# A gates' store on another queue, two transposes a block sooner, two subtractions on another engine

## The chip, the cores and the metric

The kernel runs on one core of a Trainium2 chip. Its engines have a queue of their own each and meet at semaphores: TensorE (PE; its weight loads are PEld), VectorE (DVE), ScalarE (ACT), GpSimd (POOL) and SyncE (SP), which here only issues DMAs. The metric is the device time of one execution in microseconds, as the median of several runs; less is better.

## The reference, cut to what matters

A chunked attention with a few memory keys, followed by a top-1 mixture of experts on its output.

```
attention (4 batches x 8 heads, 768 tokens, head size 64):
    for each chunk of 32 queries: keys = 8 memory keys + 16 left + own 32 + 8 right
    a = softmax(q k^T / 8);  out = a v
x = out as [3072 tokens, 512]
logits = x @ w_gate + modality_bias[modality_id];   e = argmax;   gate = softmax(logits)[e]
out[t] = gate[t] * (relu(x[t] @ w1[e]) @ w2[e])     8 experts, 512 -> 1024 -> 512
```

All of it is in float32.

## The kernel before, in words

**Attention** goes over 16 units of two heads, in two halves each, as a pipeline: scores, softmax, product with the values, transposes of the result (`xT`) for the router. The results go to a DRAM copy `xd`, each token's gate to a DRAM table `gd`. The router (`route`, one generator per batch of 768 tokens) finds each token's expert and rank and builds a table of the tokens in the order of experts. Its steps are pumped in between other work.

**Experts** are done in slots of 256 tokens of one expert. A slot gathers its rows by indirect DMA on GpSimd's queue (`gather`, `fetch`: first the rows from `xd`, then the gates from `gd`), transposes them on TensorE (`trans`: eight transposes in two sets; ScalarE casts the high part `xth`, VectorE subtracts for the low part `xtl`, L822 and L823), and multiplies twice. Each float32 product is made of three products of rounded parts: high x high, low x high, high x low. For that each block of 128x512 weights is split by `conv`: ScalarE casts the high part (L758), VectorE subtracts it from the raw weights for the low part (L759). A slot has 8 blocks of the first matrix (`raw[0..7]`) and 8 of the second (`raw[8..15]`).

`mm1_first(f)` is block f of the first product: 12 matmuls into a PSUM bank, then ScalarE's ReLU (L848) and VectorE's low part (L849). Banks come in turn from a pool of four (`bank()`); the eight blocks of slot 1 with the router's table product before block 7 take nine of them, so block 5 takes block 1's bank, block 6 block 2's, the table product block 3's and block 7 block 4's. `mm2(f)` is block f of the second product, 6 matmuls.

Slots 0 and 1 take the experts chosen after three batches, so that their work starts before the fourth batch is routed. The rest of that routing (the generator `last`, stepped by `further`) is laid between slot 0's and slot 1's blocks. It plans the slots on VectorE (`plan_slots`, its last step writes `regs1`), gets `ac` and `lo`, and then makes one-hot rows (L673, L676): for the first four of six groups on GpSimd, the others on VectorE.

**The order is the order of the code.** Each engine runs its instructions in the order in which the program was written; there is no scheduler. An instruction waits at the head of its queue, and what is behind it waits too.

**Weight loads** (`load_w(row, half)`) are issued by SP, eight at a time, into the raw buffers; they wait for the buffers to be read out by `conv`. Each carries a condition: where the expert is that of the slot before, it is issued but moves nothing. Slot 1 starts with

```
def slot(s):
    load_w(s + 1, 0)              # slot 2's first matrix, buffers 0 to 7
    ...
    for f in range(8):
        mm1_first(f)
        if f < 3: conv(5 + f)     # blocks 5 to 7 of slot 1's first matrix
        further(2)
        if f < 6: conv(8 + f)
```

so its conversions of blocks 5 to 7 stand behind slot 2's loads into these buffers; blocks 0 to 4 are converted in slot 0's second product.

Of the kernel before, what the change touches and what calls it, by code (L numbers as in the profile page):

```python
# [45 lines left out]
def tile_chunk_attention_top1_moe(  # L46
# [14 lines left out]
    nc = tc.nc  # L61
# [22 lines left out]
    def bank():  # L84
        return ps.tile([P, 512], F32, name="tr", tag="tr", bufs=4)
# [293 lines left out]
    def store_x(u):  # L379
        b, g = divmod(u, 4)  # L380
        nc.gpsimd.dma_start(xd[b * S:(b + 1) * S, g * P:(g + 1) * P].rearrange("(t p) c -> p t c", p=P), xbs[u])
# [135 lines left out]
    chosen = []  # L517
# [181 lines left out]
    def second():  # L699
        cb, eb, oha, top, ia, ib = chosen  # L700
        nc.vector.tensor_scalar(oha, rev[:, 0], ia, None, op0=ALU.is_equal)
        yield "v"
        nc.vector.tensor_scalar(top, top, 511.5, 2.0 * EMPTY, op0=ALU.is_gt, op1=ALU.mult)
        yield "v"
        nc.vector.tensor_scalar(top, top, -EMPTY, None, op0=ALU.add)
        yield "v"
        nc.vector.scalar_tensor_tensor(cb, oha, top, cb, op0=ALU.mult, op1=ALU.add)
        yield "v"
        yield from first_of(cb, top, ib, eb)
        nc.vector.tensor_scalar(ohg, rev[:, 0], ib, None, op0=ALU.is_equal)  # L710
        yield "v"
        nc.vector.tensor_scalar(noth, rev[0:64, 0], ib[0:64], None, op0=ALU.not_equal)
        yield "v"
        nc.vector.tensor_add(used, oha[0:64], ohg[0:64])
        yield "v"
        nc.vector.scalar_tensor_tensor(col0u, used, 2.0, col0, op0=ALU.mult, op1=ALU.add)
        yield "v"
        nc.vector.tensor_scalar(regsb[:, 0:1], ib[0:1], -1.0, float(E), op0=ALU.mult, op1=ALU.add)
        yield "v"
        nc.vector.tensor_tensor(regsb[:, 1:2], ia[0:1], ib[0:1], op=ALU.not_equal)  # L720
        yield "v"
        nc.vector.tensor_tensor(top[0:1], ia[0:1], ib[0:1], op=ALU.is_equal)
        yield "v"
        nc.vector.tensor_scalar(top[0:1], top[0:1], 2.0, float(E * HI), op0=ALU.mult, op1=ALU.add)
        yield "v"
        nc.vector.scalar_tensor_tensor(regsb[:, 2:3], ib[0:1], -float(HI), top[0:1], op0=ALU.mult, op1=ALU.add)
        yield "v"
# [8 lines left out]
    def load_w(row, half, part=None):  # L736
        if half == 0 and part in (None, 0):
            if row == 0:
                ev[0] = nc.values_load(regs0[0:1, 0:1], engines=[mybir.EngineType.SP], min_val=0, max_val=E - 1,
                                       skip_runtime_bounds_check_because="the place of one of 8 experts")  # L740
            else:
                r = regsb if row == 1 else (regs1 if row < NSURE else regs)[row:row + 1]
                ev[row] = nc.values_load(r[:, 0:1], engines=[mybir.EngineType.SP], min_val=0, max_val=E - 1,
                                         skip_runtime_bounds_check_because="the place of one of 8 experts, or 0")
                ev[row, "c"] = nc.values_load(r[:, 1:2], engines=[mybir.EngineType.SP], min_val=0, max_val=1,
                                              skip_runtime_bounds_check_because="a comparison gives 0 or 1")
        e = ev[row]
        kw = {} if row == 0 else {"cond": ev[row, "c"]}
        for f in range(8) if part is None else range(4 * part, 4 * part + 4):
            if half == 0:  # L750
                nc.sync.dma_start(
                    raw[f].rearrange("p (c f) -> p c f", f=P),
                    w1[ds(e, 1), :, f * P:(f + 1) * P].rearrange("o (c p) f -> p (o c) f", p=P), **kw)
            else:
                nc.sync.dma_start(raw[8 + f], w2[ds(e, 1), f * P:(f + 1) * P, :].rearrange("o p d -> p (o d)"), **kw)

    def conv(i, eng=None):
        nc.scalar.copy(wh[i], raw[i])  # L758
        (eng or nc.vector).tensor_sub(wl[i], raw[i], wh[i].bitcast(F32))  # L759
# [6 lines left out]
    def fetch(rows, part):  # L766
        for t in range(2):
            nc.gpsimd.indirect_dma_start(  # L768
                out=xg[t][:, part], out_offset=None, in_=rows, in_offset=bass.IndirectOffsetOnAxis(ap=gx[:, t:t + 1], axis=0))

    def gather(row, gates=True, between=()):
        if row < 2:
            src, reg, rows = table, regsb[0:1, 2:3] if row else regs0[0:1, 1:2], N - S
        else:
            src, reg, rows = tab_i, (regs1 if row < NSURE else regs)[row:row + 1, 2:3], N
        col = nc.values_load(reg, engines=[mybir.EngineType.Pool], min_val=0, max_val=E * HI,
                             skip_runtime_bounds_check_because="clamped to the table on chip")
        nc.gpsimd.tensor_copy(ix, src[:, ds(col, 2)])
        nc.gpsimd.tensor_scalar(gx, ix, float(rows - 1), None, op0=ALU.min)
        fetch(xd[0:rows], slice(0, DM))  # L780
        for step in between:
            step()
        if flipped(row):
            for t in range(2):
                flip(planes[t], xg[t], xpl[:, :, t * P:(t + 1) * P])
        if gates:
            fetch(gd[0:rows], slice(DM, XW))
# [27 lines left out]
    def trans(half):  # L815
        t = bank().rearrange("p (c n) -> p c n", c=2)
        for cc in range(2):
            for tt in range(2):
                c = 2 * half + cc
                nc.tensor.transpose(t[:, cc, tt * P:(tt + 1) * P], xg[tt][:, c * P:(c + 1) * P], ident)  # L820
        sl = slice(2 * half, 2 * half + 2)
        nc.scalar.copy(xth[:, sl], t)  # L822
        nc.vector.tensor_sub(xtl[:, sl], t, xth[:, sl].bitcast(F32))  # L823
# [148 lines left out]
    for i in range(n + 2):  # L972
# [118 lines left out]
        if (u, hf) == (NU - 2, 1):  # L1091
            c_ld.close()
            xp = ctx.enter_context(tc.tile_pool(name="xp", bufs=1, side="right"))
            ix = xp.tile([P, 2], I32, name="ix")
            gx = xp.tile([P, 2], I32, name="gx")
            xg = [xp.tile([P, XW], F32, name=f"xg{t}") for t in range(2)]
            xt = xp.tile([P, 4, 2, 256], F32R, name="xt")
            xth, xtl = xt[:, :, 0], xt[:, :, 1]
            w1h, w1l = [xp.tile([P, 8, 512], F32R, name=f"w1{i}") for i in range(2)]
            hh, hl = [xp.tile([P, 8, 256], F32R, name=f"h{i}") for i in range(2)]  # L1100
            for f in range(8):
                raw[f] = xp.tile([P, 512], F32, name=f"raw{f}")
                wh[f], wl[f] = w1h[:, f], w1l[:, f]
            flat = vws[1].rearrange("p h c d -> p (h c d)"), kbds[0].rearrange("p c h m -> p (c h m)")
            old = [t[:, k * 512:(k + 1) * 512] for t in flat for k in range(6)]
            raw[8:16] = old[0:8]
            load_w(0, 0, 0)
            gather(0, gates=False)
            for f in range(4, 8):
                nc.gpsimd.memset(raw[f][0:1, 0:1], 0.0)  # L1110
            load_w(0, 0, 1)
            with nc.allow_non_contiguous_dma(reason="one gate per token"):
                nc.sync.dma_start(*chosen.pop())
        elif (u, hf) == (NU - 1, 1):
            other = second()
            for f in range(8, 16):
                nc.gpsimd.memset(raw[f][0:1, 0:1], 0.0)
            load_w(0, 1)
            store_x(NU - 3)
            fetch(gd[0:N - S], slice(DM, XW))  # L1120
            store_x(NU - 2)
# [20 lines left out]
    def further(k=99, pe=False):  # L1142
        if at_pe[0] and not pe:
            return
        at_pe[0] = False
        while k > 0 and not at_pe[0]:
            at_pe[0] = next(last, "full") == "full"
            k -= 1
# [22 lines left out]
    for f in range(8):  # L1171
        if f == 2:
            further(2, True)
        mm2("av", f)
        if f < 5:
            conv(11 + f)
        if f == 5:
            load_w(1, 1)
        if f in (5, 6):
            trans(f - 5)  # L1180
        if f > 2:
            further(2)
            conv(f - 3)
    store(0)

    tails = plan_tails()
# [155 lines left out]
```

## Time and profile before

| | us |
|---|---|
| median of 3 runs (lowest, highest) | 428.49 (427.87, 429.13) |
| the profiled execution | 428.21 |
| its span, first to last instruction | 426.4 |
| PE busy | 409.3 (96%) |
| PEld busy | 341.7 (80%) |
| DVE busy | 336.3 (79%) |
| ACT busy | 299.0 (70%) |
| POOL busy | 238.5 (56%) |

Times in the rows count from the span's start. Attention fills the first 133 us; slot 0 runs from there to 161, slot 1 to 186, the other ten slots to 398. Busy shares are averages: what bounds a stage is read from the waits in that stage. In a row of the timeline the bracket is the idle time of the engine before it and what ended it.

### The profile page before, as it was taken

Reading aid. Unit: us, or ns where it says so; the run is one execution under the profiler, and the core shown is the slowest. Engines: PE = TensorE matmul, PEld = TensorE weight load, DVE = VectorE, ACT = ScalarE, POOL = GpSimd, SP = SyncE. Lnnn points to the kernel's source line nnn. Section 1 sums busy time; section 2 is a strip of 40 time slices with the busy share of each in tenths; the row PEclk is TensorE's granted clock in tenths of the full one; section 3 lists DMA queues with packets and bytes.
Section 4 is the critical chain, followed back from the end, with each engine's and each line's share of the span. In section 5 each row is a group of like instructions: output and inputs, shape, how many; then the busy total and the mean of one; then the engine's idle time right before and its main releaser. Section 6 shows DMA issues by size and latency. Waiting matters only on the chain.

```text
span 426.4 us, 11406 instructions
## 1 busy us (share of the span) xinstructions
PE 409.3 (96%) x3876; PEld 341.7 (80%) x3876; DVE 336.3 (79%) x796; ACT 299.0 (70%) x594; POOL 238.5 (56%) x320
## 2 busy tenths in 40 slices
PE   7997989999999999999999999999999999999994
PEld 4886777788767878899898888888888878888883
DVE  6889589688787788948979889767989787978750
ACT  7785868687675547557666697858878677878750
POOL 8956879669671628767753672453766076420101
PEclk9999999999999999999999999999999999999998
DMA  9788999999859710334422749959957423410101
GB/s 223 157 216 208 243 265 202 258 246 209 189 147 218 247 31 2 99 100 65 98 88 52 276 118 271 332 162 305 297 209 230 87 72 83 92 59 2 50 3 55
DMA packets 82543, 66.81 MB, mean 157 GB/s; under 512 B 50659, under 2 KB 71339, under 8 KB 82476
## 3 DMA queue, kind: packets, MB, share of 16 engines
q1 hardware_dynamic: 75276, 46.36, 45.0%
q0 software_dynamic: 6784, 19.50, 15.1%
q8 instruction: 33, 0.54, 0.6%
q14 instruction: 34, 0.28, 0.2%
q10 hardware_dynamic: 416, 0.13, 0.1%
HBM read 84.64 MB, written 12.76 MB: 228 GB/s over the span
## 4 chain that ended last, share of the span: by engine, by line
PE 52%; issue 18%; POOL 10%; DMA 10%; DVE 4%; ACT 4%; POOLq 1%; SPq 0%; ACTq 0%
PE tr L847 11%; PE sc L859 8%; PE av L859 7%; PE av L363 4%; POOL xg L768 4%; DMA out_dram<-o,ix_now 4%; PE tr L828 4%; PE sc L334 3%; ACT kbd L326 3%; PE tr L388 2%; POOL planes L793 2%; PE tr L831 2%; PE tr L298 2%; DMA vw<-in_v_dram 2%; PE tr L351 2%
## 5 line engine op out<-in xcount | busy, mean ns | idle before, releaser
L828 PE MATMUL tr<-xt,w 128*128 128x512 f32 x256 | 70.1, 395 | 0.0
L759 DVE TENSOR_TENSOR w<-raw,w 128x512 fp32r<-128x512 f32 x96 | 66.3, 735 | 4.0 <-ACT w L758 3.6
L859 PE MATMUL av<-wh,h 128*128 128x512 f32 x192 | 62.4, 398 | 0.0
L273 POOL COPY vw<-vw 24x1472 f32<-24x1472 f32 x31 | 44.1, 1423 | 21.1 <-DMA vw<-in_v_dram 19.9
L758 ACT CAST w<-raw 128x512 fp32r<-128x512 f32 x96 | 53.9, 624 | 1.5 <-DMA raw<-in_moe_w_dram 1.5
L859 PE MATMUL sc<-wh,h 128*128 128x512 f32 x160 | 51.7, 397 | 0.0
L828 PEld LDWEIGHTS tr<-xt,w 128*128 128x128 f32 x256 | 44.3, 188 | 7.3 <-DVE wl L840 0.8
L847 PE MATMUL tr<-xt,w 128*128 128x256 f32 x384 | 48.0, 284 | 0.7 <-DVE xt L823 0.7
L847 PEld LDWEIGHTS tr<-xt,w 128*128 128x128 f32 x384 | 46.8, 191 | 2.0 <-DVE xt L823 0.9
L326 ACT COPY kbd<-tr 64x672 f32<-64x672 f32 x57 | 44.6, 782 | 3.1 <-PE tr L320 1.5
L831 PEld LDWEIGHTS tr<-xt,w 128*128 128x128 f32 x256 | 39.2, 188 | 5.5
L859 PEld LDWEIGHTS av<-wh,h 128*128 128x128 f32 x192 | 36.1, 188 | 8.4 <-issue 0.2
L864 POOL DMA_INDIRECT out_dram<-o,ix_now x22 | 25.4, 1155 | 30.6 <-ACT o L863 25.2
L831 PE MATMUL tr<-xt,w 128*128 128x256 f32 x256 | 40.7, 281 | 0.0
L837 DVE TENSOR_TENSOR hs<-tr,hs 128x256 f32<-128x256 f32 x64 | 26.8, 419 | 16.6 <-ACT hs L834 14.5
L859 PE MATMUL av<-wl,h 128*128 128x512 f32 x96 | 38.1, 397 | 0.0
L838 ACT ACTIVATE h<-hs 128x256 fp32r<-128x256 f32 x64 | 26.8, 418 | 15.0 <-DVE hs L837 12.4
L768 POOL DMA_INDIRECT xg<-gd,gx x24 | 28.4, 1183 | 14.9 <-DMA gd<-gt 9.3
L859 PEld LDWEIGHTS sc<-wh,h 128*128 128x128 f32 x160 | 30.1, 188 | 7.2 <-issue 0.2
L840 DVE TENSOR_TENSOR wl<-vw,wh 128x512 fp32r<-128x512 f32 x48 | 33.2, 692 | 2.2
L841 DVE SCALAR_TENSOR_TENSOR h<-hs,h 128x256 fp32r<-128x256 f32 x64 | 28.6, 447 | 7.7 <-ACT h L838 6.8
L353 ACT ACTIVATE PT<-tr 128x384 f32<-128x384 f32 x32 | 15.8, 493 | 25.2 <-PE tr L351 25.0
(267 smaller groups left out, 914.1 us busy)
## 6 DMA issues: line engine op xcount, KB each, us to landing
raw<-in_moe_w_dram SPq DMA_DIRECT2D x96, 256.0 KB
vw<-in_moe_w_dram SPq DMA_DIRECT2D x72, 256.0 KB
k<-in_k_dram SPq DMA_DIRECT2D x16, 384.0 KB
q<-in_q_dram SPq DMA_DIRECT2D x16, 384.0 KB
xd<-xb POOLq DMA_DIRECT2D x16, 384.0 KB
kbd<-in_moe_w_dram SPq DMA_DIRECT2D x24, 256.0 KB
vw<-in_v_dram SPq DMA_DIRECT2D x32, 184.0 KB
xall<-in_moe_w_dram SPq DMA_DIRECT2D x4, 1024.0 KB
```

Source lines behind the costliest of these rows:

```text
L273: copy(vw[r0:r0 + 24, h, 1:NCH, 0:D], vw[r0 + 32:r0 + 56, h, 0:NCH - 1, 0:D])
L326: copy(dst.rearrange("p c (i j) -> p c i j", j=2)[:, :, :, j], win)
L758: nc.scalar.copy(wh[i], raw[i])
L759: (eng or nc.vector).tensor_sub(wl[i], raw[i], wh[i].bitcast(F32))
L768: nc.gpsimd.indirect_dma_start(out=xg[t][:, part], out_offset=None, in_=rows, in_offset=bass.IndirectOffsetOnAxis(ap=gx[:, t:t + 1], axis=0))
L828: nc.tensor.matmul(ph, wh[f][:, c * P:(c + 1) * P], xt[:, c].rearrange("p a n -> p (a n)"), start=(c == 0), stop=False, skip_group_check=True)
L831: nc.tensor.matmul(ph[:, 0:256], wl[f][:, c * P:(c + 1) * P], xth[:, c], start=False, stop=(c == 3), skip_group_check=True)
L837: nc.vector.tensor_add(hs, ph[:, 0:256], hs)
L840: nc.vector.tensor_sub(wl[w], raw[w], wh[w].bitcast(F32))
L841: nc.vector.scalar_tensor_tensor(hl[:, f], hs, 0.0, hh[:, f].bitcast(F32), op0=ALU.max, op1=ALU.subtract)
L847: nc.tensor.matmul(ph, w[f][:, c * P:(c + 1) * P], x[:, c, :], start=(n == 0), stop=(n == 11))
L859: nc.tensor.matmul(pos[t], x, w[8 + f], start=(f == 0 and n == 0), stop=(f == 7 and n == 2))
```

## The change

Three edits. In the last but one unit of attention the store of the third batch's gates to `gd` is issued by GpSimd and no longer by SP. In slot 0's second product slot 1's two sets of transposes come behind blocks 4 and 5, before behind blocks 5 and 6. And the subtractions that give the low parts of slot 1's weight blocks 1 and 3 are GpSimd's, no longer VectorE's.

```
                 load_w(0, 0, 1)
                 with nc.allow_non_contiguous_dma(reason="one gate per token"):
-                nc.sync.dma_start(*chosen.pop())
+                nc.gpsimd.dma_start(*chosen.pop())
...
         if f == 5:
             load_w(1, 1)
-        if f in (5, 6):
-            trans(f - 5)
+        if f in (4, 5):
+            trans(f - 4)
         if f > 2:
             further(2)
-            conv(f - 3)
+            conv(f - 3, nc.gpsimd if f in (4, 6) else None)
```

`conv(i, eng)` takes the engine for the subtraction as its second argument; the cast stays ScalarE's.

How the change stands in the engines' order. On GpSimd, between slot 1's row fetches and the fourth batch's gates; `raw_2596` to `raw_2603` are raw buffers 0 to 7, `w_2592` and `w_2593` the high and low parts. Before:

```order
L768 DMA xg_2590<-gd,gx 128x4
L673 TENSOR_SCALAR l_3172<-iota_147,lo 128x130
L676 TENSOR_SCALAR a_3173<-iota_148,ac,tokm 128x192
L673 TENSOR_SCALAR l_3176<-iota_147,lo 128x130
L676 TENSOR_SCALAR a_3177<-iota_148,ac,tokm 128x192
L628 DMA gd<-gt 128x6x4
```

and in the changed kernel:

```order
L768 DMA xg_2590<-gd,gx 128x4
L759 TENSOR_TENSOR w_2593<-raw_2597,w_2592 128x512
L673 TENSOR_SCALAR l_3179<-iota_147,lo 128x130
L676 TENSOR_SCALAR a_3180<-iota_148,ac,tokm 128x192
L673 TENSOR_SCALAR l_3183<-iota_147,lo 128x130
L676 TENSOR_SCALAR a_3184<-iota_148,ac,tokm 128x192
L759 TENSOR_TENSOR w_2593<-raw_2599,w_2592 128x512
L628 DMA gd<-gt 128x6x4
```

Block 1's subtraction stands ahead of the one-hot rows, block 3's behind the first four of them. On SP, slot 2's loads into raw buffers 2 to 5, with the queues whose semaphores they wait for. Before:

```order
L751 DMA raw_2598<-in_moe_w_dram 128x4x128 [waits DMAHW1_49,DVE_49]
L751 ISA
L751 DMA raw_2599<-in_moe_w_dram 128x4x128 [waits DMAHW2_49,DVE_49]
L751 ISA
L751 DMA raw_2600<-in_moe_w_dram 128x4x128 [waits DMAHW3_49,DVE_49]
L751 ISA
L751 DMA raw_2601<-in_moe_w_dram 128x4x128 [waits DMAHW4_49]
```

and in the changed kernel:

```order
L751 DMA raw_2598<-in_moe_w_dram 128x4x128 [waits DMAHW0_49,DVE_49]
L751 ISA
L751 DMA raw_2599<-in_moe_w_dram 128x4x128 [waits DMAHW1_49,Pool_49]
L751 ISA
L751 DMA raw_2600<-in_moe_w_dram 128x4x128 [waits DMAHW2_49,DVE_49]
L751 ISA
L751 DMA raw_2601<-in_moe_w_dram 128x4x128 [waits DMAHW3_49]
```

The load into buffer 3 waits for GpSimd and no longer for VectorE, and the loads into 4 and 5 are behind it. On VectorE, around the plan of the slots (`ng` to `sta`), the difference:

```order
 L759 TENSOR_TENSOR wl_2863<-kbd_110,wh_2862 128x512
+L823 TENSOR_TENSOR xt<-tr,xt 128x2x256
 L461 TENSOR_REDUCE ng<-own 64x1
 L462 TENSOR_SCALAR ng<-ng 64x1
...
 L468 TENSOR_TENSOR sta<-sta,noth 64x8
-L759 TENSOR_TENSOR w_2593<-raw_2597,w_2592 128x512
 L823 TENSOR_TENSOR xt<-tr,xt 128x2x256
 L470 SCALAR_TENSOR_TENSOR sta<-ohg,sta 64x8
```

The first low half of the rows now stands ahead of the plan, the second in its middle, where the first one was.

## Rows read from the trace of the kernel before

**Rows 1.** The page's busy times: engine, us, share of the span, instructions.

```profile
PE 409.3 (96%) x3876; PEld 341.7 (80%) x3876; DVE 336.3 (79%) x796; ACT 299.0 (70%) x594; POOL 238.5 (56%) x320
```

**Rows 2.** Stretches: length, then PE PEld DVE ACT POOL busy, clock, DMA, GB/s.

```profile
133.70:161.00 27.30, 27.26 (x200) 23.14 (x193) 22.35 (x79) 14.62 (x33) 10.17 (x13) 1.00 0.50 139
161.00:163.00 2.00, 1.26 (x12) 1.06 (x10) 1.90 (x8) 1.48 (x3) 1.25 (x2) 1.00 0.00 0
163.00:174.40 11.40, 11.40 (x93) 11.28 (x94) 10.50 (x25) 7.01 (x16) 10.86 (x13) 1.00 0.10 26
174.40:398.00 223.60, 223.60 (x1329) 189.04 (x1328) 183.75 (x362) 164.95 (x347) 114.70 (x142) 1.00 0.53 146
```

**Rows 3.** Timeline of PE: start, us, engine, line, operation, count, idle before.

```profile
157.21 0.60 PE L820 MATMUL tr<-ident,xg 128*128 128x128 f32 x4
...
160.89 1.34 PE L847 MATMUL tr<-xt,w 128*128 128x256 f32 x10
162.97 9.14 PE L847 MATMUL tr<-xt,w 128*128 128x256 f32 x74 [0.74 <-DVE xt L823]
171.95 0.82 PE L684 MATMUL tr<-a,l 128*128 128x192 f32 x6
172.72 1.70 PE L847 MATMUL tr<-xt,w 128*128 128x256 f32 x12
```

**Rows 4.** Timeline of ACT and DVE around the rows' halves and the plan.

```profile
157.90 0.59 ACT L822 CAST xt<-tr 128x512 fp32r<-128x512 f32 x1 [4.83 <-PE tr L820]
158.52 0.69 DVE L823 TENSOR_TENSOR xt<-tr,xt 128x512 fp32r<-128x512 f32 x1 [1.15 <-ACT xt L822]
...
161.56 0.16 DVE L646 TENSOR_TENSOR ac<-c,hi 128x6 f32<-128x6 f32 x1
...
162.24 0.68 DVE L823 TENSOR_TENSOR xt<-tr,xt 128x512 fp32r<-128x512 f32 x1
...
163.14 0.70 DVE L759 TENSOR_TENSOR w<-raw,w 128x512 fp32r<-128x512 f32 x1
```

**Rows 5.** Timeline of SP: slot 2's loads into raw buffers 3, 4, 5.

```profile
163.87 0.07 SPq L751 DMA_DIRECT2D raw<-in_moe_w_dram  x1
...
164.84 0.07 SPq L751 DMA_DIRECT2D raw<-in_moe_w_dram  x1
...
165.23 0.07 SPq L751 DMA_DIRECT2D raw<-in_moe_w_dram  x1
```

**Rows 6.** Timeline of ACT and DVE in slot 1, blocks 5, 1 and 4.

```profile
165.36 0.62 ACT L758 CAST w<-raw 128x512 fp32r<-128x512 f32 x1 [1.46 <-DMA raw<-in_moe_w_dram]
...
166.02 0.69 DVE L759 TENSOR_TENSOR w<-raw,w 128x512 fp32r<-128x512 f32 x1 [0.86 <-ACT w L758]
...
167.87 0.42 DVE L849 SCALAR_TENSOR_TENSOR h<-tr,h 128x256 fp32r<-128x256 f32 x1
...
172.25 0.42 DVE L849 SCALAR_TENSOR_TENSOR h<-tr,h 128x256 fp32r<-128x256 f32 x1
```

**Rows 7.** Timeline of POOL: the first, fourth and last of eight one-hot rows.

```profile
161.75 1.06 POOL L673 TENSOR_SCALAR l<-iota,lo 128x130 fp32r<-128x130 f32 x1 [9.36 <-DVE ac L646]
...
164.40 1.30 POOL L676 TENSOR_SCALAR a<-iota,ac,tokm 128x192 fp32r<-128x192 f32 x1
...
169.41 1.33 POOL L676 TENSOR_SCALAR a<-iota,ac,tokm 128x192 fp32r<-128x192 f32 x1
```

**Rows 8.** Groups of POOL by shape: count, busy us, mean ns of one, idle before.

```profile
L273 POOL COPY vw<-vw 24x1472 f32<-24x1472 f32 x31 | 44.1, 1423 | 21.1 <-DMA vw<-in_v_dram 19.9
...
L676 POOL TENSOR_SCALAR a<-iota,ac,tokm 128x192 fp32r<-128x192 f32 x10 | 11.3, 1131 | 0.0
...
L248 POOL TENSOR_TENSOR rows_b<-bias_b,ident 24x192 f32<-24x192 f32 x1 | 0.5, 505 | 0.1
...
L246 POOL TENSOR_TENSOR bias_b<-bias_b 24x8 f32<-24x8 f32 x1 | 0.2, 196 | 0.0
```

**Rows 9.** Waits from 120 to 200 us: us in total, times, longest.

```profile
POOL xg L768 <- DMA gd<-gt: 9.3, 1, 9.3
```

## The prediction

> **What bounds the kernel now.** I read the page's first part, then the table of stretches, and only then the rows around the change. TensorE's row on the page has 409.3 us busy of 426.4 [rows 1]. A matmul's end is modelled, so that row alone proves little; the stretches say more. From 133.7 to 161 us TensorE has 27.26 of 27.30 us busy, from 163 to 174.4 all of 11.40, and from 174.4 to 398 all of 223.60, at a granted clock of 1.00 [rows 2]. Between them, from 161 to 163, it has 1.26 of 2.00: a hole of 0.74 us, the only one from the start of the expert slots to the last one's end. The reader is to see two things in this. A gain here can come only from that hole (and 0.04 us before it). And nothing behind 174.4 can absorb a delay: what slot 1 loses arrives at the end of the kernel.
>
> The timeline of TensorE shows what the hole is: slot 1's first block starts at 160.89, runs 10 matmuls and then waits 0.74 us for VectorE's `xt`, line 823 [rows 3]. This is the low half of the second pair of row transposes. VectorE starts it at 162.24, although ScalarE's half was ready long before, because in its own order the plan of the slots (up to `ac`, at 161.56) and a weight subtraction stand in front [rows 4].
>
> **The two sets of transposes, one block sooner.** They leave one place and enter another: 8 transposes and 24 matmuls in another order, no instruction more. The first set goes from 157.21 to one block sooner, about 155.8, and the second to about 157.6, that is where the first stood plus the first's own 0.4 us. ScalarE took 0.69 us from the start of a set to its cast (157.21 to 157.90) and VectorE another 0.62 (158.52) [rows 3, 4]. So the last low half now starts at 157.6 + 0.69 + 0.62 = 158.9 and is done by 159.6, before TensorE asks for it, at 162.97 - 0.74 = 162.2 [rows 3]. The hole closes: -0.74 us. What is late next? The plan rows used to follow the first `xt`, which started at 158.52; now they follow the second, at 158.9. So `ac` ends at 161.72 + 0.4 = 162.1, and GpSimd's one-hot rows, which wait for it, start 0.4 us later. The gathered rows should be there: GpSimd had issued all of slot 1's fetches by 161.75 - 9.36 = 152.4 [rows 7], 3.4 us before the new place.
>
> **The subtraction of block 1 (f = 4) on GpSimd.** VectorE loses one 0.70 us instruction. On GpSimd it stands in front of the one-hot rows, where GpSimd idled 9.36 us [rows 7]. It can run when ScalarE has cast the high half, about 157.7 (the first set's cast ends at 156.5 + 0.6, and its own cast takes 0.6), and is over by 160.7 even at the dearest price below. TensorE reads block 1's low part 16 matmuls behind 160.89, at about 162.8. Cost zero; the cover is GpSimd's idle time before `ac`, and it ends at 162.1.
>
> **The subtraction of block 3 (f = 6) on GpSimd.** This is the one that counts. It stands behind the first four one-hot instructions, and those wait for `ac`. Before, VectorE did it at 163.14, done at 163.84 [rows 4]. Now the four rows start at 162.1; they took from 161.75 to 165.70 [rows 7], of which I take back 0.05 because two of VectorE's subtractions beside them are gone, so the subtraction starts at 166.0.
>
> Its price is not in the trace at this size. GpSimd's two-operand rows took 196 ns at 8 elements and 505 at 192 [rows 8]: 309 ns for 184 more elements, 1.68 ns each, so 505 + 320 x 1.68 = 1.04 us at 512. Bounds: at the pace of its plain copy (1423 ns for 1472 elements) 0.5 us; at the pace of its two-scalar row (1131 ns for 192) 3.0 us [rows 8]. I take 1.04, the rows of the same operation. It ends at T = 167.05 (166.5 to 169.0).
>
> The Trainium skill, GPSIMD Engine Reference, section 3.1, speaks against this edit: it has a two-operand add on GpSimd at 1.96 times VectorE's time, 4497 ns for 2048 elements; a quarter is an estimate of 1.12 us. By that page the sum below would be 0.1 us longer; no run here shows the operation at this size yet.
>
> Who waits for it? Two. First TensorE: it reads that block's low half 40 matmuls after 160.89. With 74 matmuls in 9.14 us [rows 3] one is 0.123, so at 165.8; it would stall 1.3 us. Second, and longer, SP. Slot 2's weight loads go into the same raw buffers in the order 0 to 7, and the load into buffer 3 now waits for GpSimd. In the trace that load is issued at 163.87, right behind VectorE's 163.84; then 164.84 (behind subtraction 4) and 165.23, so 0.39 us from one free load to the next [rows 5]. ScalarE's cast of block 5 for slot 1 stands behind the load into buffer 5: its row waits 1.46 us for a DMA into `raw` and starts at 165.36, 0.13 after that load's issue [rows 6]. That the loads move next to nothing (26 GB/s in the stretch [rows 2]) doesn't help: the wait is for their turn. Now the issues are at 167.08, 167.47 and 167.86, and the cast starts at 167.99 (T + 0.94): 2.63 us late.
>
> What is queued behind this cast? ScalarE's next casts and ReLUs, in order, and VectorE's subtraction 5 (166.02 before), from which VectorE runs without a gap to the low half of block 4, 172.25 + 0.42 = 172.67 [rows 6]. Blocks share four PSUM banks, and block 7 takes the one that block 4 leaves: in the trace TensorE starts block 7 at 172.72 [rows 3], 0.05 after that. VectorE has no gap there to give up, so all of it moves by 2.63, and block 7 starts at 175.35. TensorE's stalls on the way (1.3 at block 3, 1.4 at block 5 for block 1's bank, freed by the row at 167.87, the rest at blocks 6 and 7) are parts of this and not added to it: it arrives at block 7 2.63 us late, net of the 0.74 gained.
>
> GpSimd's second pair of one-hot rows ended at 170.74 with TensorE asking at 171.95 [rows 3, 7]; both move by about the same (1.35 and over 2), so this costs nothing.
>
> **The gates' store on GpSimd's queue.** SP loses one issue; GpSimd gains one, in front of the touches of the buffers that SP loads next. GpSimd waited 9.3 us for this store to land before it could fetch slot 0's gates [rows 9]; part of that goes, and the stores of attention's last rows behind the fetch start sooner. But TensorE had 0.04 us to gain in the 27 us that follow [rows 2], which is the bound below zero. A loss would need SP's next loads to come later by the touches than they came by SP's own issue, which is gone; I see none and cost the edit at 0.
>
> **Sum.** +2.63 against the profiled execution's 428.21 is 430.8. The median of the runs shown is 428.49, 0.28 more, so I forecast 431.1 us. With the price's bounds the delay is 2.1 to 4.6.
>
> **Rivals.** A: the load's wait is not on the path (block 7 doesn't need what it looks like), and only TensorE's own wait for block 3 counts: 1.3 - 0.74 = +0.6, 429.1 us. For it: block 7 and the end of block 4's row stand 0.05 apart, which could be chance. Against: ScalarE's wait for the DMA is named in the trace. B, the other side: GpSimd's subtraction is done in time and the hole's 0.74 us is gained, 427.8 us. It decides at T = 165.36 - 0.94 = 164.4, so the one-hot rows would have to be over by 163.4, 2.3 us sooner than in the trace; against it is their wait for `ac`. For it: VectorE is freed of two subtractions of 0.70. C: GpSimd needs 3.0 us as in its slowest row, T = 169.0, +4.6, 433.1 us. For it: its rows beside VectorE's subtractions are stretched (1.30 against a mean of 1.13); against: VectorE's next subtraction itself waits on this one, so it runs alone.
>
> The Trainium skill, SBUF — State Buffer, "Who interferes with whom", calls the port that GpSimd shares with VectorE an exclusive lock, taken against two-input VectorE instructions. The row of 1.30 us agrees; were one to come ahead of subtraction 3, the sum would grow by its 0.70 us, to 431.8.
>
> **How the numbers follow.** Forecast (delay of 1.6 to 3.4 us) 0.68, A 0.12, B 0.06, C and in between 0.14. From no change this kernel can be told at about 0.3%, 1.3 us: A lies within it, and so does B unless VectorE's relief adds half a microsecond more, to which I give 0.04 of its 0.06. So faster 0.04, same 0.14, slower 0.82. The range, 429.3 to 432.9, leaves out B, half of A and the far end of C.
>
> **What would show it.** In the profile of the changed kernel: no wait for `xt` before slot 1's third group; GpSimd's subtraction 3 between 166 and 167.2; SP's load into buffer 3 right behind it; ScalarE's cast of block 5 at about 168.0 with a longer wait for `raw`; TensorE's stretch from 163 to 177 with some 3 us idle, at blocks 3 and 5 above all; and from there everything 2.6 later. Wrong if that cast starts before 166, or if TensorE reaches slot 1's second product (174.26 before) in under 1.3 us more.

## The result and the profile after

The changed kernel takes 430.36 us (median of 22 runs, 428.94 to 434.88), the kernel before beside it 428.33 (22 runs, 425.75 to 431.01). The ratio of the runs is 1.0073, with a 95% interval of [1.0054, 1.0092]: about 3.1 us more (2.3 to 3.9). The two medians stand 2.03 apart, so the size is known to about 1 us only. The forecast was 2.63 more. All ratios here leave out, as slow, a run over 1.5% above the fastest of its kernel: two of experiment 9 (432.54 and 433.36 us) and one of the kernel before (1374.79).

The profiled execution took 433.25 us, its span is 431.5. This is not the number to compare: its first matmul of the experts comes at 135.72, before at 133.76, so 1.96 us were lost in attention, ahead of everything that the change touches in the experts. They are not the change's: in this execution TensorE waits 1.64 us up to 78.03 us, and behind that the granted clock is 0.50, the lower of its two levels (1.2 GHz), for 3.4 us (78.5 to 81.9); the trace before has no such stretch in attention, and the first of the three edits comes some 50 us later. Over the twelve traces of this document that first matmul comes between 130.61 and 136.09. I compare from the first matmul of slot 0's second product to that of slot 1's second product: 29.03 us (150.02 to 179.05) against 26.20 (148.06 to 174.26), 2.83 more. The page's busy times, to be laid beside [rows 1], tell little:

```profile
PE 411.1 (95%) x3876; PEld 342.4 (79%) x3876; DVE 338.2 (78%) x794; ACT 300.0 (70%) x594; POOL 237.6 (55%) x323
```

Stretches of the changed kernel: slot 0, slot 1's first product, the rest (columns as in [rows 2]).

```profile
135.70:162.40 26.70, 26.70 (x195) 23.11 (x192) 22.21 (x73) 15.37 (x33) 11.09 (x14) 1.00 0.47 154
162.40:179.05 16.65, 13.28 (x103) 12.45 (x102) 12.31 (x36) 7.86 (x18) 12.89 (x15) 1.00 0.11 34
179.05:403.00 223.95, 223.95 (x1331) 189.34 (x1330) 185.72 (x362) 165.65 (x347) 110.82 (x141) 1.00 0.52 145
```

All of the loss is in the middle one: 16.65 us with 3.37 idle. Behind it TensorE is busy throughout, so nothing gives the time back. TensorE there, the answer to [rows 3]:

```profile
162.41 4.94 PE L847 MATMUL tr<-xt,w 128*128 128x256 f32 x40
168.97 2.66 PE L847 MATMUL tr<-xt,w 128*128 128x256 f32 x20 [1.62 <-POOL w L759]
173.13 1.70 PE L847 MATMUL tr<-xt,w 128*128 128x256 f32 x12 [1.50 <-DVE h L849]
175.05 1.70 PE L847 MATMUL tr<-xt,w 128*128 128x256 f32 x12 [0.22 <-DVE h L849]
176.58 0.91 PE L684 MATMUL tr<-a,l 128*128 128x192 f32 x6
177.52 1.69 PE L847 MATMUL tr<-xt,w 128*128 128x256 f32 x12
179.05 0.39 PE L859 MATMUL sc<-wh,h 128*128 128x512 f32 x1
```

The 0.74 us for `xt` are gone. In their place stand 1.62 behind 40 matmuls, for GpSimd's subtraction of block 3, then 1.50 and 0.22 at blocks 5 and 6, for VectorE's rows that free their banks. GpSimd, the answer to [rows 7]:

```profile
159.20 1.28 POOL L759 TENSOR_TENSOR w<-raw,w 128x512 fp32r<-128x512 f32 x1 [7.39 <-ACT w L758]
164.05 1.06 POOL L673 TENSOR_SCALAR l<-iota,lo 128x130 fp32r<-128x130 f32 x1 [3.56 <-DVE ac L646]
...
166.69 1.00 POOL L676 TENSOR_SCALAR a<-iota,ac,tokm 128x192 fp32r<-128x192 f32 x1
167.67 1.25 POOL L759 TENSOR_TENSOR w<-raw,w 128x512 fp32r<-128x512 f32 x1
```

GpSimd waits 3.56 us for `ac`, does four one-hot rows, and only then the subtraction that TensorE and SP want. It ends at 168.92. SP's loads into buffers 3, 4 and 5 [rows 5] and the casts and subtractions behind them [rows 6]:

```profile
168.94 0.07 SPq L751 DMA_DIRECT2D raw<-in_moe_w_dram  x1
169.36 0.07 SPq L751 DMA_DIRECT2D raw<-in_moe_w_dram  x1
169.75 0.07 SPq L751 DMA_DIRECT2D raw<-in_moe_w_dram  x1
```

```profile
169.88 0.62 ACT L758 CAST w<-raw 128x512 fp32r<-128x512 f32 x1 [5.46 <-DMA raw<-in_moe_w_dram]
...
170.47 1.00 POOL L676 TENSOR_SCALAR a<-iota,ac,tokm 128x192 fp32r<-128x192 f32 x1
...
170.53 0.97 DVE L759 TENSOR_TENSOR w<-raw,w 128x512 fp32r<-128x512 f32 x1 [4.06 <-ACT w L758]
...
177.06 0.41 DVE L849 SCALAR_TENSOR_TENSOR h<-tr,h 128x256 fp32r<-128x256 f32 x1
```

The issues come 0.02, 0.44 and 0.83 us behind the end of GpSimd's subtraction, the cast 0.96 behind it (forecast 0.03, 0.42, 0.81 and 0.94). Counted from slot 1's start (160.89 before, 162.41 now), the cast of block 5 starts at 7.47 us; before at 4.47. VectorE in the changed kernel, the answer to [rows 4]:

```profile
158.63 0.69 DVE L823 TENSOR_TENSOR xt<-tr,xt 128x512 fp32r<-128x512 f32 x1 [1.33 <-ACT xt L822]
...
159.60 0.91 DVE L463 TENSOR_TENSOR_SCAN end<-oth,ng 64x8 f32<-64x8 f32 x1
...
160.83 0.68 DVE L823 TENSOR_TENSOR xt<-tr,xt 128x512 fp32r<-128x512 f32 x1
...
163.86 0.16 DVE L646 TENSOR_TENSOR ac<-c,hi 128x6 f32<-128x6 f32 x1
```

and one row of the same view of the kernel before:

```profile
156.14 0.23 DVE L463 TENSOR_TENSOR_SCAN end<-oth,ng 64x8 f32<-64x8 f32 x1
```

Two things: both low halves are early enough, and `ac` ends 1.61 us after slot 1's start, before 0.83: +0.78 where the forecast had +0.4. The scan, a row of 8 elements, took 0.91 and not 0.23. It ends at 160.51, with GpSimd's subtraction of block 1 (160.48).

The gates' store: GpSimd's wait for it fell from 9.3 [rows 9] to

```profile
POOL xg L768 <- DMA gd<-gt: 4.1, 1, 4.1
```

and slot 0's second product took 12.39 us (150.02 to 162.41), before 12.83. So more was to be had here than the 0.04 of the forecast, in this trace; the experiments show that it does not hold in every trace with the store there.

### The profile page after: what moved, and what is told of

Read it like the earlier page. It is cut to its first block, busy times and chain, and to the rows that moved or that the text cites. A ratio compares the mean times of both kernels' runs of the same rounds, so it can differ in the third digit from the quotient of the medians.

```text
span 431.5 us, 11406 instructions
## 1 busy us (share of the span) xinstructions
PE 411.1 (95%) x3876; PEld 342.4 (79%) x3876; DVE 338.2 (78%) x794; ACT 300.0 (70%) x594; POOL 237.6 (55%) x323
## 4 chain that ended last, share of the span: by engine, by line
PE 36%; issue 14%; POOL 5%; DMA 3%; DVE 1%; POOLq 1%; ACT 0%; DVEq 0%; ACTq 0%
PE sc L859 10%; PE av L859 8%; PE tr L828 7%; PE tr L847 6%; PE tr L831 4%; DMA out_dram<-o,ix_now 3%; POOL xg L768 2%; POOL planes L793 1%; POOL out_dram L864 1%; POOL out_dram L1272 0%; PE tr L921 0%; PE tr L906 0%; DVE wl L759 0%; POOLq L1197 0%; POOL ix_now L762 0%
## 5 line engine op out<-in xcount | busy, mean ns | idle before, releaser
L840 DVE TENSOR_TENSOR wl<-vw,wh 128x512 fp32r<-128x512 f32 x48 | 34.8, 725 | 2.1
L841 DVE SCALAR_TENSOR_TENSOR h<-hs,h 128x256 fp32r<-128x256 f32 x64 | 26.9, 420 | 7.7 <-ACT h L838 7.7
L834 ACT COPY hs<-tr 128x256 f32<-128x256 f32 x64 | 23.6, 369 | 13.0 <-PE tr L831 9.6
```

Source lines behind the costliest of these rows:

```text
L840: nc.vector.tensor_sub(wl[w], raw[w], wh[w].bitcast(F32))
L841: nc.vector.scalar_tensor_tensor(hl[:, f], hs, 0.0, hh[:, f].bitcast(F32), op0=ALU.max, op1=ALU.subtract)
```

## The experiments

My theory was the forecast's: GpSimd's subtraction of block 3 is late because it stands behind rows that wait for the plan; SP's loads wait for it in turn; block 5's cast waits for the loads; VectorE is late with the bank of block 7. Against it: it is the gates' store; or GpSimd as such; or only TensorE's own wait for block 3. Each was run beside the kernel before, in five rounds. Beside the ratio each tells two stretches of its trace: slot 0's second product and slot 1's first product (before 12.83 and 13.37; changed 12.39 and 16.64).

**1. Only the gates' store** (on the kernel before).

```
-                nc.sync.dma_start(*chosen.pop())
+                nc.gpsimd.dma_start(*chosen.pop())
```

> The kernel before with the gates' store alone on GpSimd's queue. I measure one stretch in the trace: from the first matmul of slot 0's second product to the first of slot 1's second product (26.20 us before, 29.03 with the whole change), and the time. Theory (the cost is GpSimd's subtraction 3 through SP's loads): no delay from this edit; the stretch 25.8 to 26.2, since ScalarE's first cast of slot 0's second matrix no longer waits for the row stores; the time within 0.5 us of before. Rival (the store on GpSimd is what costs): the stretch or the time before it grows by 1 us or more.

Ratio 1.0030 [1.0006, 1.0054], about 1.3 us more; 13.44 and 13.36, in sum 26.80. My theory is missed in both numbers, and the rival's 1 us is met in the time, not in the stretch (0.60 more). Slot 1 is as before, with its wait of 0.75 for `xt` and block 5's cast at 4.48. Slot 0 got longer, not shorter: one ReLU of ScalarE waited for something that the profile only calls remote.

```profile
151.28 0.38 ACT L848 ACTIVATE h<-tr 128x256 fp32r<-128x256 f32 x1 [1.27 <-remote]
```

So the edit has nothing to do with the loss in slot 1, but costing it at 0 wasn't safe either.

**2. Only the transposes** (on the kernel before).

```
-        if f in (5, 6):
-            trans(f - 5)
+        if f in (4, 5):
+            trans(f - 4)
```

> The kernel before with the transposes alone one block sooner; all subtractions stay on VectorE. Theory with the chain: the 0.74 us hole before slot 1's third group closes, but block 7 goes on waiting for the bank that VectorE frees behind the cast of block 5, so the stretch from slot 0's to slot 1's second product stays at 25.9 to 26.2 us and the wait turns up at blocks 5 to 7. Rival (my sum: the hole's 0.74 us is a gain of its own): the stretch falls to 25.4 to 25.5 us.

Ratio 1.0024 [0.9997, 1.0050]; 12.79 and 13.47, in sum 26.26: just over the theory's 25.9 to 26.2, and far from the rival's 25.4 to 25.5. TensorE, and VectorE's second low half and `ac`:

```profile
161.57 7.34 PE L847 MATMUL tr<-xt,w 128*128 128x256 f32 x60
169.11 1.69 PE L847 MATMUL tr<-xt,w 128*128 128x256 f32 x12 [0.20 <-DVE h L849]
171.03 1.70 PE L847 MATMUL tr<-xt,w 128*128 128x256 f32 x12 [0.23 <-DVE h L849]
172.66 0.95 PE L684 MATMUL tr<-a,l 128*128 128x192 f32 x6
```

```profile
159.90 0.68 DVE L823 TENSOR_TENSOR xt<-tr,xt 128x512 fp32r<-128x512 f32 x1
...
162.94 0.16 DVE L646 TENSOR_TENSOR ac<-c,hi 128x6 f32<-128x6 f32 x1
```

The hole is closed, and the product is no shorter: from its start to the table product 11.09 us (161.57 to 172.66), before 11.06 (160.89 to 171.95, [rows 3]). Stops at blocks 5 and 6, held by VectorE's rows, took the hole's place. (A stop costs more than its bracket, which counts from the modelled end of the last matmul: 12 matmuls at 0.123 are 1.48 us, and their row says 1.69 or 1.70.) The hole was no gain to be had alone. And `ac` ends 1.53 us after slot 1's start, 0.70 later than before, by the transposes alone.

**3. The change with block 3's subtraction back on VectorE.**

```
-            conv(f - 3, nc.gpsimd if f in (4, 6) else None)
+            conv(f - 3, nc.gpsimd if f == 4 else None)
```

> The changed kernel with subtraction 3 back on VectorE (subtraction 1 stays on GpSimd). Theory: the loss goes; ScalarE's cast of block 5 starts 4.2 to 4.7 us after slot 1's first matmul (4.47 before, 7.47 with the whole change), the stretch is 25.5 to 26.3 us, the time that of before. Rival (contention of GpSimd and VectorE at the shared port, or subtraction 1, makes the loss): the stretch stays above 27.5 us.

Ratio 1.0006 [0.9975, 1.0037]; 13.58 and 13.55. TensorE's wait behind 40 matmuls is gone:

```profile
160.42 7.35 PE L847 MATMUL tr<-xt,w 128*128 128x256 f32 x60
168.05 1.69 PE L847 MATMUL tr<-xt,w 128*128 128x256 f32 x12 [0.28 <-DVE h L849]
```

One subtraction of 1.25 us carries nearly the whole loss of slot 1: 16.64 falls to 13.55 (13.37 before), block 5's cast starts at 4.65 and not at 7.47, and the time is that of before. The sum of both stretches, 27.13, is not the 25.5 to 26.3 expected: slot 0's product is 1.19 longer than in the changed kernel, behind a wait of ScalarE for "remote" (2.01 us) as in experiment 1. Block 1's on GpSimd costs next to nothing: `ac` ends 1.61 after slot 1's start and the product takes 13.55, with it on VectorE (experiment 2) 1.53 and 13.47.

**4. The change, with slot 2's load into buffer 3 issued last of the eight.**

```
-        for f in range(8) if part is None else range(4 * part, 4 * part + 4):
+        for f in (0, 1, 2, 4, 5, 6, 7, 3) if (row, half) == (2, 0) else range(8) if part is None else range(4 * part, 4 * part + 4):
```

> The changed kernel with slot 2's loads issued in the order of buffers 0, 1, 2, 4, 5, 6, 7, 3, so that the load that waits for GpSimd's subtraction 3 stands last; nothing else differs. Theory (the wait goes through SP's queue): the cast of block 5 starts 4.0 to 4.6 us after slot 1's first matmul and no longer 7.47; TensorE's own wait for block 3's low half stays (1.5 us), the waits at blocks 5 to 7 go; the stretch is 26.3 to 27.0 us, 2 to 2.7 less than with the whole change. Rival (only TensorE's own wait for block 3 counts): the stretch stays at 29.0 us.

Ratio 1.0069 [1.0043, 1.0095]; 13.56 and 15.76. The chain through SP is shown in the trace: the subtraction is as late as ever, and block 5's cast starts at 4.28 and not at 7.47; the waits at blocks 5 and 6 are gone. The time did not follow, though, and the sum of both stretches is 29.32, the rival's number (29.0) and not the theory's (26.3 to 27.0). TensorE, and stretches behind its wait:

```profile
159.53 4.94 PE L847 MATMUL tr<-xt,w 128*128 128x256 f32 x40
166.33 7.02 PE L847 MATMUL tr<-xt,w 128*128 128x256 f32 x44 [1.86 <-POOL w L759]
```

```profile
166.30:167.30 1.00, 0.97 (x5) 0.97 (x5) 1.00 (x3) 1.00 (x3) 0.95 (x2) 0.56 0.03 8
167.30:168.30 1.00, 1.00 (x6) 1.00 (x6) 1.00 (x3) 0.27 (x1) 1.00 (x2) 0.50 0.36 12
168.30:169.30 1.00, 1.00 (x7) 1.00 (x6) 1.00 (x3) 0.89 (x2) 1.00 (x1) 0.50 0.00 0
169.30:170.50 1.20, 1.20 (x10) 1.20 (x10) 1.20 (x3) 0.00 (x0) 1.20 (x2) 0.77 0.00 0
170.50:172.00 1.50, 1.50 (x15) 1.50 (x15) 1.50 (x4) 0.94 (x3) 1.50 (x2) 1.00 0.00 0
```

Behind the wait of 1.86 us the granted clock is 0.50, the lower of its two levels (1.2 GHz), until about 170. The 44 matmuls took 7.02 us; at the pace of the 40 ahead of the wait (4.94) they take 5.43. So 1.59 of this product's 2.39 us over before is the clock, and 0.80 is what rival A priced at 0.6: TensorE's own wait. The rest of the 29.32 is slot 0's product (13.56, with a wait for "remote" of 2.00). So this product is still 0.88 shorter than the changed kernel's (15.76 for 16.64), by another mixture; what SP's turn costs alone, in time, this run does not show. That the clock fell here and stayed at 1.00 behind the changed kernel's 1.62 is what the rows show; it is one trace, and why is open.

**5. The change, block 3's subtraction written behind block 5's conversion.**

```
+            if f == 6: conv(3, nc.gpsimd)
             further(2)
-            conv(f - 3, nc.gpsimd if f in (4, 6) else None)
+            if f != 6: conv(f - 3, nc.gpsimd if f == 4 else None)
```

> The changed kernel with GpSimd's subtraction 3 moved ahead of its first four one-hot rows, behind subtraction 1; the same three edits and the same instructions otherwise. I measure slot 1's first product in the trace, from its first matmul to the first of its second product: 13.37 us before, 16.64 with the whole change. Theory (what costs is that subtraction 3 stands behind rows that wait for the plan, not that GpSimd does it): GpSimd runs it before the plan ends, the cast of block 5 starts 4.0 to 4.9 us after the first matmul (7.47 with the whole change), no wait for block 3, the product takes 13.2 to 13.9 us and the time falls back to within 1.5 us of before. Rival (a subtraction on GpSimd costs by its own length or by the shared port): the product stays above 15 us.

Ratio 1.0099 [1.0065, 1.0134]; 12.39 and 16.66. A miss in the design: the four one-hot rows are already issued in block 5's `further(2)`, so the subtraction passed nothing. What is left is a second sample of the change, with the same waits.

**6. The change with the gates' store back on SP.**

```
-                nc.gpsimd.dma_start(*chosen.pop())
+                nc.sync.dma_start(*chosen.pop())
```

> The changed kernel with the gates' store back on SP; transposes and both subtractions as in the change. Theory: slot 1's first product is as slow as with the whole change, 16.3 to 16.9 us, or slower by up to 1.3 where TensorE's clock is lowered behind its wait for block 3; slot 0's second product takes 12.8 us as before, and not 13.4 to 13.6 as in three of the four kernels with the store on GpSimd's queue. The time is then 0.5 to 1 us under that of the whole change. Rival (the store is a good part of the loss): slot 1's first product falls under 15.5 us.

Ratio 1.0093 [1.0066, 1.0121]; 12.85 and 16.66. TensorE's waits in slot 1 are those of the changed kernel:

```profile
167.11 2.65 PE L847 MATMUL tr<-xt,w 128*128 128x256 f32 x20 [1.63 <-POOL w L759]
171.26 1.69 PE L847 MATMUL tr<-xt,w 128*128 128x256 f32 x12 [1.50 <-DVE h L849]
```

The rival of the gates' store falls. The 0.5 to 1 us that I expected this run to be under the whole change is missed too: its ratio is no lower than the change's 1.0073.

**7. and 8. Slot 2's loads into buffers 4 to 7 issued behind the conversions of blocks 5 to 7**, on the kernel before alone (7) and with the transposes a block sooner (8, the edit of experiment 2 added).

```
-            load_w(s + 1, 0)
+            load_w(s + 1, 0, 0 if s == 1 else None)
...
+                if f == 2:
+                    load_w(s + 1, 0, 1)
```

> The kernel before with only slot 2's loads into buffers 4 to 7 issued behind slot 1's conversions of blocks 5 to 7. Theory of two walls: the first wall, TensorE's 0.74 us for the low half of the rows, is untouched, so slot 1's first product stays at 13.2 to 13.4 us and the time is that of before. Rival (the cast of block 5 alone bounds this product): it falls to 12.6 to 12.9 us.

> The kernel before with the transposes a block sooner, and slot 2's loads into buffers 4 to 7 issued behind slot 1's conversions of blocks 5 to 7, no longer ahead of them; all subtractions on VectorE, the gates' store on SP. Theory (two walls stand behind each other, the low half of the rows at 162 us and the cast of block 5 behind SP's loads): with both gone slot 1's first product takes 12.6 to 12.9 us, 0.5 to 0.75 less than before, the cast of block 5 starts under 3.5 us after the first matmul and no wait is left at blocks 5 to 7; the time is 0.5 to 0.8 us under before, at the edge of what can be told. Rival (the waits at blocks 5 to 7 are VectorE's own load of work, not the loads' order): 13.3 to 13.5 us, as with the transposes alone.

7: ratio 1.0015 [0.9997, 1.0033]; 12.66 and 13.18. Block 5's cast starts at 2.93, the hole of 0.75 stays. 8: ratio 1.0003 [0.9983, 1.0024]; 12.63 and 13.39. The cast starts at 1.91, hole and waits at blocks 5 to 7 are all gone, and still nothing is gained: my 12.6 to 12.9 are missed, and the rival's number (13.3 to 13.5) came for another reason than its own. What is late next is new, the table product, split by a wait for GpSimd's last one-hot row:

```profile
169.24 0.55 PE L684 MATMUL tr<-a,l 128*128 128x192 f32 x3
170.62 0.58 PE L684 MATMUL tr<-a,l 128*128 128x192 f32 x3 [0.83 <-POOL a L676]
```

Slot 1's first product has at least three walls of nearly one height: the hole, SP's turn, GpSimd's rows. Taking two away shows the third.

**9. The change with block 3's subtraction ahead of the one-hot rows**, what experiment 5 meant to be.

```
         if f > 2:
+            if f == 5:
+                conv(3, nc.gpsimd)
             further(2)
-            conv(f - 3, nc.gpsimd if f in (4, 6) else None)
+            if f != 6:
+                conv(f - 3, nc.gpsimd if f == 4 else None)
```

> The changed kernel, with block 3's subtraction still GpSimd's but written one block sooner, ahead of block 5's step of the routing and so ahead of the first four one-hot rows. Theory (it is the place behind the rows that wait for the plan which costs, by SP's in-order queue): GpSimd's second subtraction follows the first, at about 160 to 162 us, over 4 us sooner; slot 2's load into buffer 3 no longer stands in the way, ScalarE's cast of block 5 starts 4.2 to 5.0 us into slot 1 (7.47 in the changed kernel, 4.47 before), the first product of slot 1 takes 13.2 to 14.2 us (16.64 and 13.37), and the time is within 0.4% of the kernel before. Rival 1 (a subtraction on GpSimd is what costs, wherever it stands): first product of 16 us or more, ratio over 1.005. Rival 2 (two subtractions in a row on GpSimd hold VectorE's plan up through the shared port): ac ends 2 us or more into slot 1 (0.83 before, 1.61 in the changed kernel), the one-hot rows come late, and the table product before block 7 waits for GpSimd; first product of 14.2 to 15.5.

Ratio 1.0005 [0.9975, 1.0036]; 13.06 and 13.94. GpSimd, VectorE's row of the plan beside it, ScalarE's cast of block 5:

```profile
160.23 1.29 POOL L759 TENSOR_TENSOR w<-raw,w 128x512 fp32r<-128x512 f32 x1 [8.36 <-ACT w L758]
162.06 1.30 POOL L759 TENSOR_TENSOR w<-raw,w 128x512 fp32r<-128x512 f32 x1 [0.55 <-ACT w L758]
```

```profile
162.45 0.93 DVE L470 SCALAR_TENSOR_TENSOR sta<-ohg,sta 64x8 f32<-64x8 f32 x1
...
168.49 0.62 ACT L758 CAST w<-raw 128x512 fp32r<-128x512 f32 x1 [3.05 <-DMA raw<-in_moe_w_dram]
```

The same work on the same engine, one block sooner, and the cast starts at 5.06 (expected up to 5.0) and not 7.47; of the 3.27 us lost in slot 1's first product 2.70 are back. It was the place. Rival 2 is half right: the second subtraction holds a row of the plan as the first held the scan (0.93 us; it ends at 163.38 with GpSimd's at 163.36), and `ac` ends 2.39 after slot 1's start. But the table product doesn't wait for it: TensorE waits 0.69 and 0.22 us, both for VectorE's `h`.

**10. Experiment 8 with the last routing's fourth one-hot group on VectorE.**

```
-        npool = 4 if b == B - 1 else NPOOL
+        npool = 3 if b == B - 1 else NPOOL
```

> The transposes a block sooner and slot 2's loads into buffers 4 to 7 behind the conversions of blocks 5 to 7, everything else as in the kernel before; new: the last routing's fourth group of one-hot rows is VectorE's and no longer GpSimd's. Theory (three walls in slot 1's first product: the hole at the first block, SP's queue at blocks 5 to 7, GpSimd's one-hot rows ahead of the table product): the wait of 0.83 us that the table product had with four groups on GpSimd goes, the first product takes 12.6 to 12.9 us (13.39 with four groups, 13.37 before), and the time is 0.3 to 0.8 us less than before, at the edge of what can be told: ratio 0.998 to 1.000. Rival (VectorE is the wall and the two more rows there move block 4's low part late): the first product stays at 13.2 to 13.6, and TensorE waits for VectorE's h or one-hot rows instead.

Ratio 0.9998 [0.9967, 1.0028]; 13.03 and 13.13. Between both expectations: the wait for GpSimd is gone, and a shorter one for VectorE stands there.

```profile
159.93 10.46 PE L847 MATMUL tr<-xt,w 128*128 128x256 f32 x84
170.69 0.88 PE L684 MATMUL tr<-a,l 128*128 128x192 f32 x6 [0.31 <-DVE h L849]
```

It beats the kernel before by nothing that can be measured. No version here does.

## Why the prediction was right, point by point

**The bound and the missing slack.** Right. The loss arrived at the end: 3.27 us more in slot 1's first product, 0.44 less in slot 0's second, 2.83 in the traces, 1.0073 [1.0054, 1.0092] in the runs, against a forecast ratio of 1.0061 (2.63 of 428.21). That 2.83 and 2.63 stand so close is partly luck: slot 1's loss was forecast 0.64 too small, and slot 0's 0.44, which the forecast did not have, hides most of that. One sentence of it is wrong: that a gain can come only from the idle time. Slot 0 had 0.04 us of it and got 0.44 shorter. Ends of matmuls are modelled, and short stops do not show as idle time: the first matmul of slot 0's second product starts 0.43 us ahead of the next in the kernel before, 0.23 in the changed one, and neither row has a bracket.

**Block 3's subtraction and SP's turn.** The mechanism was right in each link, as experiments 3 (without that subtraction no loss), 4 (without SP's order no late cast) and 9 (the same subtraction in another place, no loss that can be measured) show. Experiments 3 and 9 show it in the time as well; 4 shows it in the trace alone, because there the clock took what the order gave back. How the loss divides between SP's turn and TensorE's own wait is not shown. Its size was 0.64 short, in these terms:

- The end of the subtraction, counted from slot 1's start: 6.51 us, forecast 6.16. `ac` came 0.38 later than forecast; the four rows took 3.62 (164.05 to 167.67) and not 3.90, which gives 0.28 back; the subtraction took 1.25 and not 1.04; 0.03 lie between `ac` and the first row. The Trainium skill, GPSIMD Engine Reference, section 3.1, had led to an estimate of 1.12; both estimates are under the row.
- From the cast to block 7 the forecast moved everything by the same amount. VectorE's subtraction of block 5 took 0.97 and not 0.69 [rows 6], beside a one-hot row of GpSimd (170.47 to 171.47). This is the last 0.28.

**The transposes.** The step that was reasoned wrongly. It let the second low half start at 158.9, right behind ScalarE, 0.4 us behind where the first one stood. In the kernel before, the plan's first rows filled VectorE's wait for the first low half (the 1.15 us idle in [rows 4] is what was left of it); now that half comes first, and the second stands behind those rows. With the transposes alone `ac` is 0.70 later (experiment 2).

**Block 1's subtraction, at zero.** VectorE was relieved of 0.6 us between two starts, and the scan took 0.68 more: +0.70 became +0.78. Zero was near, but for two terms that cancel; the forecast named the first and carried neither to `ac`. The Trainium skill, SBUF — State Buffer, "Who interferes with whom", speaks of an exclusive lock on a port that GpSimd and VectorE share, for two-input work of VectorE. The traces agree: the scan took 0.91 or 0.92 us in all six kernels with this subtraction on GpSimd (changed, experiments 3, 4, 5, 6 and 9), 0.23 in all six without (before, experiments 1, 2, 7, 8 and 10). I had this lock in the forecast, but only over block 3's subtraction and not over block 1's.

**The hole as 0.74 netted.** Right as written: the delay at block 7 counts, and the hole is part of the way there. Rival B, in which it is a gain, falls: even with GpSimd's subtraction of block 3 away (experiments 2 and 3) the first product takes 13.47 and 13.55, no less than 13.37.

**Rival A** was not what happened in the changed kernel, but its price was real: 0.80 in experiment 4 without the clock's part. **Rival C** had the slowest row as price: 3.0 us; it is 1.25.

**The gates' store at 0.** Not settled. The bound of 0.04 was too narrow: slot 0's second product took 12.39 in two traces with the store on GpSimd (the changed kernel, experiment 5) and 13.06 to 13.58 in four (experiments 1, 3, 4 and 9); 12.63 to 13.03 in the six with it on SP. Alone it cost 1.0030 [1.0006, 1.0054]; taken out of the change it gained nothing (experiment 6). The longer four are those in which ScalarE's ReLU behind the router's `rex` waited for "remote", 1.27 to 2.44 us. By the traces' semaphore records that ReLU waits for TensorE's own signal for block 7 of slot 0's first product. The signal comes 2.05 to 2.55 us behind the modelled end of the block's last matmul in these four, 0.60 in the changed kernel, and at most 0.18 in experiment 5 and in the six with the store on SP. Why it is late was not found.

## What to carry to other kernels

Before work is given to an idle engine, look at what stands ahead of it in that engine's order: GpSimd idled 3.56 us and was still late, since it idled in front of rows that waited for something else; one block sooner the same edit cost nothing that could be measured. Follow the buffer as well as the result: whoever reads a raw buffer last sets when the next load may be issued, and on a queue that runs in order one late load holds all behind it, even loads that move next to nothing. And a hole is worth its length only if nothing else ends just behind it: here two walls were taken away and a third stood there.

## What the runs showed of the hardware that was not expected

- Three VectorE rows with two inputs that started while a GpSimd row was under way took longer and ended within 0.04 us of it: the scan of 8 elements 0.91 for 0.23 us, another row of 8 elements 0.93 in experiment 9 (0.15 in the kernel before), a subtraction of 512 elements 0.97 for 0.69. Elsewhere the GpSimd row was the one that grew: 1.30 us in [rows 7], beside VectorE's subtraction at 164.14, which kept its 0.68. Two rows with one input beside the same GpSimd row (`ng`, 0.14 and 0.15 us) were not held.
- The granted clock at 0.50 from 167.3 to 169.3 in experiment 4, behind 1.86 us without a matmul: 1.59 us more for 44 matmuls. Behind 1.62 us in slot 1 of the changed kernel it stayed at 1.00; behind 1.64 us in attention, in the same trace, it was 0.50 for 3.4 us. What decides is not shown.
